# Weights' float64 words turned into float32 by a parametric ReLU on ScalarE, one shift and one OR

## The chip, the cores and the metric

The kernel runs on one core of a Trainium2 chip. The metric is the device time in microseconds of one launch. The time before is the median of three runs.

## The reference, cut to what matters

Sigmoid attention over 8 batches of 12 heads (448 positions, head width 64), then a two-layer perceptron over the 3584 tokens:

```
scores = matmul(q, k^T) / sqrt(64) - log(448)
x      = matmul(sigmoid(scores), v)          # 8 x 448 tokens, 768 wide
h      = x @ w_in                            # 768 -> 2048
g      = h where h >= 1; 0 where h <= -1; (h + 1)^2 / 4 between
out    = g @ w_out                           # 2048 -> 768
```

The two weight matrices reach the kernel as float64. The kernel computes in float32 and in pairs of float16 (a high and a low half), and so has to turn each float64 weight into a float32 first. A float64 is two 32-bit words. The high one holds the sign, 11 bits of exponent and 20 bits of mantissa; the low one's top three bits are the last that a float32 keeps.

## The kernel before, in words

**Stages.** The batches `b` follow each other. Each has six head pairs, and each pair four pieces (three blocks of 128 keys and a half block), so 24 pieces a batch. Per piece TensorE makes scores (lines 407, 411, 416 and 425), ScalarE makes the sigmoid (454 or 457) and TensorE multiplies by V (498). After a batch's pieces its x is copied out (504), its maximum is found (508, 517), spread over the partitions by a small matmul (165, 175, 176) and x is scaled and split into halves (521, 522). Then come the up products of the perceptron (`up`, line 722; from batch 2 on `up_blocks`, 688), the bend of `h` into `g` (735 to 739), and the down products (`down`, 758). While one batch goes through the perceptron, the next one's attention is worked in between. The first eight pairs are multiplied as float32 and need no split; they come from `first_qvk`.

**Weights.** Each matrix is 16 chunks of 128 rows by 768 float64, that is 768 KB each. `Weight.load` (line 202) starts a chunk's transfer: w_in's on the queue of SyncE, most of w_out's on ScalarE's. w_in's raw words lie in six spare places inside w_out's buffer, so the load of chunk f+6 waits until chunk f is converted, and what stands behind it on SyncE's queue waits too. `Weight.convert` (210) is called once per step and works on three chunks: it finishes chunk f-2, begins chunk f and does the middle of chunk f-1.

- Begin: ScalarE takes the absolute value of the high word, read as a float32 (line 224). For a *summed* chunk (the even ones of w_in) a clamp follows at once (226), on GpSimd for the first four and on VectorE for the other four.
- Middle, on VectorE: for a chunk that isn't summed, the clamp of line 236 also gives the maximum by an accumulator; then two shifts in one operation (241), the OR with the low word's top bits (244), and the OR with the sign and the top exponent bit out of the high word (247).
- Finish, for the summed chunks alone: ScalarE sums absolute values into an accumulator (218), which serves as a bound of the maximum.

There are 8 summed chunks and 24 others (8 of w_in, all 16 of w_out). `find_scale` is called twice for each matrix, after half its chunks and after all: it takes the maximum over chunks (259), makes a true float32 of it (262, 265), merges the sums (269), spreads the maximum over the partitions (165, 175, 176) and sets the scale (131 to 139). `split` then makes the float16 halves of each chunk (286 and 287, or 282 to 284 with GpSimd).

**Order.** Program order gives priorities, and a scheduler places each engine's instructions by them and by its own idea of when data is ready. What each engine runs in which order is therefore fixed when the kernel is built, for all engines at once, and a change of a few instructions can move others. Each engine works through its list in order: an instruction that waits holds up all behind it.

Of the kernel before, what the change touches and what calls it, by code (L numbers as in the profile page):

```python
# [14 lines left out]
F32 = mybir.dt.float32  # L15
F16 = mybir.dt.float16
BF16 = mybir.dt.bfloat16
I32 = mybir.dt.int32
AF = mybir.ActivationFunctionType
ALU = mybir.AluOpType  # L20
AX = mybir.AxisListType
PSUM = bass.MemoryType.PSUM

P = 128
# [4 lines left out]
ATT = 2.0**14  # L29
TINY = 2.0**-60  # L30

HIGH_MIN = 1.125 * 2.0**-15

NFULL = 8
NHALF = 6

# [17 lines left out]
LSTEP = 3  # L54

SB = 2
CLAMP = 7
QA = 17
QT = 3
WOP = 6  # L60
# [15 lines left out]
def sigmoid_attention_mlp(ctx: ExitStack, tc: tile.TileContext, first_qvk, qkv, w_in, w_out, out_t):  # L76
    nc = tc.nc
    NFULL, _, _, S = first_qvk.shape
    B = out_t.shape[1] // S
    NFC, _, DM = w_out.shape  # L80
# [44 lines left out]
    def scales(m, n, tag, pool=None, square=False, less=0):  # L125

        pool = pool or sml_p
        few = {"bufs": 1} if tag == "x" else {}
        mask, top = (EXP_MASK - EXP_ONE, TOP - 1) if square else (EXP_MASK, TOP - less)
        e = sml_p.tile([P, 3], F32, tag="e", name=tag + "_e")[:, :n]  # L130
        nc.vector.tensor_scalar(out=e, in0=m, scalar1=TINY, scalar2=None, op0=ALU.max)  # L131
        ei = e.bitcast(I32)
        nc.vector.tensor_scalar(out=ei, in0=ei, scalar1=mask, scalar2=None, op0=ALU.bitwise_and)
        s = pool.tile([P, n], F32, tag=tag + "_s", name=tag + "_s", **few)
        nc.vector.tensor_scalar(
            out=s.bitcast(I32), in0=ei, scalar1=-1.0, scalar2=float((2 * 127 + top) * EXP_ONE), op0=ALU.mult, op1=ALU.add
        )
        inv = pool.tile([P, n], F32, tag=tag + "_i", name=tag + "_i", **few)
        nc.vector.tensor_scalar(  # L139
            out=inv.bitcast(I32), in0=ei, scalar1=float(top * EXP_ONE), scalar2=None, op0=ALU.subtract  # L140
        )
        return s, inv
# [7 lines left out]
        out=ident, in_=ident, pattern=[[-1, P]], compare_op=ALU.is_equal, fill=0.0, base=0, channel_multiplier=1  # L150
# [17 lines left out]
    def all_max(m, diag=None):  # L168

        if diag is None:  # L170
            diag = on_diagonal(m)
            pm = ps_mo.tile([P, 512], F32, tag="mo", name="pm")
        else:
            pm = ps_sc.tile([P, 2, 512], F32, tag="psc", name="psc")[:, 0, :]
        nc.tensor.matmul(pm[:, :P], ones, diag, start=True, stop=True)
        nc.vector.tensor_reduce(out=m, in_=pm[:, :P], axis=AX.X, op=ALU.max)


    class Weight:
# [30 lines left out]
        def convert(self):  # L210

            f = self.at - 2
            if 0 <= f < NFC:
                w = self.words.pop(f)
                if f in self.summed:

                    dump = wo.f32(-1) if self is wi else w[:, :DM].bitcast(F32)
                    nc.scalar.activation(dump, self.f32(f), AF.Abs, accum_out=self.most[:, 1, f : f + 1])
                if self is wo:
                    self.load(3 if f == 3 else 1)  # L220
            f = self.at
            if f < NFC:
                a = self.f32(f)
                nc.scalar.activation(a, self.words_of(f)[1].bitcast(F32), AF.Abs)
                if f in self.summed:
                    (nc.vector if f >= CLAMP else nc.gpsimd).tensor_scalar(
                        out=a, in0=a, scalar1=HIGH_MIN, scalar2=None, op0=ALU.max
                    )
            f = self.at - 1
            if 0 <= f < NFC:  # L230

                low, high = self.words_of(f)
                a = self.f32(f)
                ai = a.bitcast(I32)
                if f not in self.summed:
                    nc.vector.tensor_scalar(
                        out=a, in0=a, scalar1=HIGH_MIN, scalar2=0.0, op0=ALU.max, op1=ALU.max,
                        accum_out=self.most[:, 0, f : f + 1],
                    )

                nc.vector.tensor_scalar(
                    out=ai, in0=ai, scalar1=5, scalar2=2, op0=ALU.logical_shift_left, op1=ALU.logical_shift_right
                )
                nc.vector.scalar_tensor_tensor(  # L244
                    out=ai, in0=low, scalar=29, in1=ai, op0=ALU.logical_shift_right, op1=ALU.bitwise_or
                )
                nc.vector.scalar_tensor_tensor(  # L247
                    out=ai, in0=high, scalar=-0x40000000, in1=ai, op0=ALU.bitwise_and, op1=ALU.bitwise_or
                )
                if self is wi:  # L250
                    self.load(1, nc.sync)
            self.at += 1

        def find_scale(self):

            k = len(self.scale)
            name = "%s%d" % (self.name, k)
            m = sml_p.tile([P, 2], F32, tag="wm", name=name + "_m", bufs=1)
            nc.vector.tensor_reduce(out=m, in_=self.most[:, :, GROUPS[k]], axis=AX.X, op=ALU.max)
            c, e = m[:, 0:1], sml_p.tile([P, 1], F32, tag="wx", name=name + "_x", bufs=1)  # L260
            ci, ei = c.bitcast(I32), e.bitcast(I32)
            nc.vector.tensor_scalar(
                out=ei, in0=ci, scalar1=5, scalar2=2, op0=ALU.logical_shift_left, op1=ALU.logical_shift_right
            )
            nc.vector.scalar_tensor_tensor(
                out=ei, in0=ci, scalar=0x40000000, in1=ei, op0=ALU.bitwise_and, op1=ALU.bitwise_or
            )

            nc.vector.tensor_scalar(
                out=e, in0=e, scalar1=float(DM // P), scalar2=m[:, 1:2], op0=ALU.mult, op1=ALU.max  # L270
            )
            all_max(e)
            s, inv = scales(e, 1, name, const, square=self is wo)
            self.scale.append(s)
            self.inv.append(inv)
# [552 lines left out]
    with tc.manual_schedule(engines={mybir.EngineType.SP}):  # L828
        load_pair(0)
        wi.load(1, nc.sync)  # L830
        load_pair(1)
        wi.load(2, nc.sync)
        load_pair(2)
        wi.load(3, nc.sync)
        for i in range(LAG):
            scores([i])
        state["scored"] = LAG
        while at < NPIECE:
            step(at)
            at += 1  # L840
            for what, when in ((load_pair, L0), (prep_a, A0), (prep_b, A0 + 1)):
                for k in range(2):
                    if at == when + LSTEP * k:
                        what(NFULL + k)
            convert(wi, min((NA + 1) * at // WI_A, NA + 1 + max(0, at - WI_A) * (NFC - NA) // (NPIECE - WI_A + WI_B)))
            if at == WI_A:
                with tc.high_priority(offset=WI_PRIO):
                    wi.find_scale()
                    wi.split(0)
                    wi.split(1)  # L850
# [7 lines left out]
    for u, unit in enumerate(units):  # L858
        while at < 2 * NPIECE and B0 + (at - NPIECE) * (B1 - B0) // NPIECE <= u:
            step(at)  # L860
            at += 1
        if wi.at < NFC + 1:
            n = NPIECE - WI_A
            convert(wi, NA + 1 + min(NFC - NA, (n + u + 1) * (NFC - NA) // (n + WI_B)))
            if wi.at == NFC + 1:
                wi.find_scale()
                group_scales(0, inv_x, 1)
        f, r = divmod(u, NCC // 2)

        assert all(at >= NPC * (p + 1) or (f + 1) * S * 4 <= slot_of(p) * 3 * S * 4 for p in range(NP, NFULL)), u  # L870
        if r == 0 and f < NFC:
            wi.split(f + AHEAD, f >= POOL_FROM)
        if wo.at < NA + 1:
            convert(wo, min(NA + 1, (u + 1) * (NA + 1) // WO_A))
            if wo.at == NA + 1:
                wo.find_scale()
                split_at = 0
        elif wo.at < NFC + 1:
            convert(wo, min(NFC + 1, NA + 1 + (u + 1 - WO_A) * (NFC - NA) // (WO_B - WO_A)))
            if wo.at == NFC + 1:  # L880
                wo.find_scale()
                roots()
        if len(wo.scale):
            while split_at < min(NA, 2 * (u + 1 - WO_A)):
                wo.split(split_at, split_at % WOP == 1)
                split_at += 1
        unit()
# [79 lines left out]
```

## Time and profile before

| | |
|---|---|
| time, three runs | 1190.55, 1190.84, 1192.1 us |
| median | 1190.84 us |
| span of the profiled execution | 1185.7 us |
| TensorE busy | 1144.9 us (97%) |
| VectorE, ScalarE, GpSimd busy | 854.9, 697.6, 332.8 us |
| mean granted TensorE clock | 0.991 |

The profile is of one execution more. Its span, from the first to the last instruction, is 1185.7 us; that execution's own device time isn't given beside it. The median stands 5.1 us above the span, which is what lies around the instructions. All sums are made against the span, and the 5.1 us are carried over as they are.

In the profile PE is TensorE (PEld its weight loads), DVE VectorE, ACT ScalarE, POOL GpSimd and SP SyncE; "L247" is line 247. A bracket at a row's end is the idle time of the engine before that row and what ended it. Operations in a row overlap a little at their ends, so that a 0.96 us operation holds the engine for some 0.87 us when the next follows directly.

### The profile page before, as it was taken

The page shows a single profiled execution, that of the slowest core. Times are in us where ns is not written, and L with a number is a line of the kernel's source. Part 1 is how long each engine was busy: PE and PEld are TensorE (multiplying, and loading weights), DVE is VectorE, ACT ScalarE, POOL GpSimd, SP SyncE. Part 2 cuts the span into 40 slices and gives each one's busy share as a digit, 9 for nine tenths or more (in the row PEclk, how much of TensorE's full clock was granted, in tenths as well). Part 3 has the DMA queues.
Part 4 walks back from the last instruction along what each step waited for, and adds up shares of the span by engine and source line. Part 5 has one row for each costly group of instructions (what it writes and reads, how often), then busy time and mean ns, then how long its engine had stood idle before and what let it go on. Part 6 is the DMA issues. An engine that isn't in the chain of part 4 may idle for free.

```text
span 1185.7 us, 20268 instructions
## 1 busy us (share of the span) xinstructions
PE 1144.9 (97%) x7662; PEld 669.3 (56%) x7662; DVE 854.9 (72%) x1828; ACT 697.6 (59%) x1158; POOL 332.8 (28%) x393
## 2 busy tenths in 40 slices
PE   5889899999999999999999999999999999999998
PEld 1224333444445776457754677557764577558954
DVE  6999999999956588457973689456884678736830
ACT  5886576665654577547864578455864476613510
POOL 3004410011323244234345235332532353310000
PEclk9899999999999999999999999999999999999999
DMA  9842354437542266224643065423552246302400
GB/s 367 322 153 76 118 161 152 134 119 257 182 148 72 95 217 210 76 72 142 238 163 102 30 236 208 135 64 128 204 211 64 65 147 220 126 24 87 163 16 32
DMA packets 58113, 170.01 MB, mean 143 GB/s; under 512 B 8608, under 2 KB 39840, under 8 KB 51872
## 3 DMA queue, kind: packets, MB, share of 16 engines
q1 hardware_dynamic: 56288, 159.29, 39.1%
q10 hardware_dynamic: 1728, 9.44, 2.2%
q8 instruction: 60, 0.98, 0.3%
q14 instruction: 37, 0.30, 0.1%
HBM read 126.94 MB, written 23.40 MB: 127 GB/s over the span
## 4 chain that ended last, share of the span: by engine, by line
PE 71%; DVE 17%; DMA 4%; ACT 3%; issue 2%; POOL 2%; SPq 0%; POOLq 0%; ACTq 0%; DVEq 0%
PE po L758 33%; PE ph L688 22%; PE pav L498 8%; PE psc L416 3%; PE psc L425 2%; PE ph L722 2%; DVE g L736 2%; PE psc L411 1%; DVE g L737 1%; DVE ghl L739 1%; DMA raw<-qkv 1%; DVE ahl L466 1%; DVE w_in_sb L244 1%; DVE mixa L632 1%; DVE w_out_sb L247 1%
## 5 line engine op out<-in xcount | busy, mean ns | idle before, releaser
L758 PE MATMUL po<-ghl,w_out_sb 128*128 128x448 f16 x2304 | 446.3, 353 | 1.5 <-DVE qkv_e L131 0.6
L758 PEld LDWEIGHTS <-w_out_sb 128*128 128x128 f16 x2304 | 221.7, 98 | 219.4 <-issue 15.9
L688 PE MATMUL ph<-w_in_sb 128*128 128x224 f16 x3024 | 307.7, 259 | 1.3 <-DVE g L737 0.9
L688 PEld LDWEIGHTS <-w_in_sb 128*128 128x128 f16 x3024 | 282.6, 98 | 30.1 <-issue 27.2
L466 DVE SCALAR_TENSOR_TENSOR ahl<-psc,ahl 128x896 f16<-128x896 f32 (+1 forms) x170 | 153.0, 900 | 105.7 <-ACT ahl L465 103.6
L378 POOL TENSOR_SCALAR raw<-raw,qkv_s 128x448 f32<-128x448 f32 (+1 forms) x93 | 71.0, 777 | 449.9 <-DVE qkv_i L139 346.3
L457 ACT ACTIVATE psc<-psc,nls,sqk 128x896 f32<-128x896 f32 (+1 forms) x136 | 129.5, 971 | 103.5 <-PE psc L425 86.6
L465 ACT ACTIVATE ahl<-psc 128x896 f16<-128x896 f32 (+1 forms) x170 | 126.9, 762 | 29.8 <-DVE ahl L466 28.6
L722 PE MATMUL ph<-xhl,w_in_sb 128*128 128x448 f16 x576 | 114.5, 356 | 4.7 <-DVE g L737 3.4
L344 ACT ACTIVATE dump<-raw 128x448 f16<-128x448 f32 (+1 forms) x105 | 61.9, 589 | 85.8 <-DMA raw<-qkv 84.5
L697 DVE TENSOR_TENSOR xhl<-ph,xhl 128x224 f32<-128x224 f32 x240 | 87.7, 383 | 25.3 <-PE ph L688 19.4
L738 ACT ACTIVATE ghl<-g 128x448 f16<-128x448 f32 x128 | 72.5, 573 | 44.2 <-DVE g L737 43.8
L498 PE MATMUL pav<-ahl,v 128*64 128x448 f16 x748 | 95.6, 360 | 0.0
L735 ACT ACTIVATE g<-xhl,hr,ihr 128x448 f32<-128x448 f32 x96 | 68.7, 752 | 41.9 <-DVE xhl L697 41.0
L722 PEld LDWEIGHTS <-w_in_sb 128*128 128x128 f16 x576 | 55.7, 99 | 63.6 <-issue 14.4
L736 DVE SCALAR_TENSOR_TENSOR g<-g,rk 128x448 f32<-128x448 f32 x112 | 81.4, 741 | 10.2 <-ACT g L735 10.0
L739 DVE TENSOR_TENSOR ghl<-g,ghl 128x448 f16<-128x448 f32 x128 | 85.0, 672 | 5.3 <-ACT ghl L738 4.8
L768 DVE TENSOR_SCALAR o<-po,od 128x448 f32<-128x448 f32 x48 | 32.5, 679 | 61.1 <-PE po L758 60.8
L380 POOL TENSOR_TENSOR hl<-raw,hl 128x448 f16<-128x448 f32 x62 | 71.1, 1167 | 0.0
L416 PE MATMUL psc<-qk 128*128 128x448 f16 x252 | 66.3, 354 | 2.0 <-ACT a L454 1.0
L737 DVE SCALAR_TENSOR_TENSOR g<-xhl,ihs,g 128x448 f32<-128x448 f32 x96 | 66.3, 708 | 0.3
L498 PEld LDWEIGHTS <-v 128*64 128x64 f16 x748 | 36.3, 109 | 37.9 <-issue 23.0
(167 smaller groups left out, 1198.5 us busy)
## 6 DMA issues: line engine op xcount, KB each, us to landing
w_in_sb<-blocks SPq DMA_DIRECT2D x48, 1344.0 KB, 6.1
raw<-qkv SPq DMA_DIRECT2D x34, 704.0 KB, 4.7
qk<-hl SPq DMA_DIRECT2D x320, 56.0 KB, 2.0
w_out_sb<-w_in SPq DMA_DIRECT2D x16, 768.0 KB, 8.5
out_t<-o SPq DMA_DIRECT2D x48, 224.0 KB, 1.9
blocks<-mixs SPq DMA_DIRECT2D x8, 768.0 KB, 3.5
w_out_sb<-w_out ACTq DMA_DIRECT2D x6, 768.0 KB, 4.1
raww<-w_out ACTq DMA_DIRECT2D x6, 768.0 KB, 5.7
```

Of the source, the lines that this page charges most:

```text
L416: nc.tensor.matmul(out, kq[:, j, 1, w], kq[:, j, 0, :], start=True, stop=False)
L457: nc.scalar.activation(a, a, AF.Sigmoid, bias=nls, scale=sqk)
L465: nc.scalar.activation(hi, x, AF.Copy, scale=ATT)
L466: nc.vector.scalar_tensor_tensor(out=lo, in0=x, scalar=ATT, in1=hi, op0=ALU.mult, op1=ALU.subtract)
L498: nc.tensor.matmul(pav[j * D : (j + 1) * D, :S], *terms[j][t], start=c == 0 and t == 0, stop=mid and t == len(terms[j]) - 1,)
L688: nc.tensor.matmul(out, w[:, wt, wh, c * P : (c + 1) * P], xc[:, xt, c, xh, :], start=j in (0, 2) and c + wh + xh == 0, stop=c == HC - 1 a ...
L697: add = lambda out, q, other: nc.vector.tensor_tensor(out=out, in0=quarter(q), in1=other, op=ALU.add)
L722: nc.tensor.matmul(ph[:, :S], w_in_sb[:, f, wh, c * P : (c + 1) * P], xhl[:, c, xh, :], start=c == 0 and wh + xh == 0, stop=c == NCC - 1 a ...
L736: nc.vector.scalar_tensor_tensor(out=g, in0=g, scalar=rt, in1=g, op0=ALU.min, op1=ALU.mult)
L737: nc.vector.scalar_tensor_tensor(out=g, in0=h, scalar=ihs, in1=g, op0=ALU.mult, op1=ALU.max)
L739: (nc.gpsimd if f % GPOOL else nc.vector).tensor_tensor(out=ghl[:, f, 1, :], in0=g, in1=hi, op=ALU.subtract)
L758: nc.tensor.matmul(po[:, :S], w_out_sb[:, f, wh, m * P : (m + 1) * P], ghl[:, f, gh, :], start=f == lo and wh + gh == 0, stop=f == hi - 1 ...
```

## The change

ScalarE's absolute value becomes a parametric ReLU with scale 2^-112 and, for negative values, the factor -2^32. For a positive weight the result's bits hold the wanted exponent and mantissa three places too low, with zeros above; for a negative one they hold a one besides, which a shift by three brings to the place of the sign. So one shift and one OR with the low word give the float32 with its sign. The clamps (lines 226 and 236) and the sign operation (247) are gone. The maximum of a chunk that isn't summed is now a reduction of its own, of absolute values, after the OR. `find_scale` finds true float32 maxima and drops two of its small operations. The sums of line 218 stay, and so do all loads and splits in program order; what the scheduler makes of it is shown in the prediction. Behind the changed part the line numbers of the changed kernel are 22 lower: line 407 of before is 385, 498 is 476, 722 is 700.

```diff
-HIGH_MIN = 1.125 * 2.0**-15
-CLAMP = 7
...
             if f < NFC:
-                a = self.f32(f)
-                nc.scalar.activation(a, self.words_of(f)[1].bitcast(F32), AF.Abs)
-                if f in self.summed:
-                    (nc.vector if f >= CLAMP else nc.gpsimd).tensor_scalar(
-                        out=a, in0=a, scalar1=HIGH_MIN, scalar2=None, op0=ALU.max
-                    )
+                high = self.words_of(f)[1].bitcast(F32)
+                nc.scalar.activation(self.f32(f), high, AF.Prelu, scale=2.0**-112, alpha=-(2.0**32))
             f = self.at - 1
             if 0 <= f < NFC:
-                low, high = self.words_of(f)
-                a = self.f32(f)
+                low, a = self.words_of(f)[0], self.f32(f)
                 ai = a.bitcast(I32)
-                if f not in self.summed:
-                    nc.vector.tensor_scalar(
-                        out=a, in0=a, scalar1=HIGH_MIN, scalar2=0.0, op0=ALU.max, op1=ALU.max,
-                        accum_out=self.most[:, 0, f : f + 1],
-                    )
-                nc.vector.tensor_scalar(
-                    out=ai, in0=ai, scalar1=5, scalar2=2, op0=ALU.logical_shift_left, op1=ALU.logical_shift_right
-                )
+                nc.vector.tensor_scalar(out=ai, in0=ai, scalar1=3, scalar2=None, op0=ALU.logical_shift_left)
                 nc.vector.scalar_tensor_tensor(
                     out=ai, in0=low, scalar=29, in1=ai, op0=ALU.logical_shift_right, op1=ALU.bitwise_or
                 )
-                nc.vector.scalar_tensor_tensor(
-                    out=ai, in0=high, scalar=-0x40000000, in1=ai, op0=ALU.bitwise_and, op1=ALU.bitwise_or
-                )
+                if f not in self.summed:
+                    nc.vector.tensor_reduce(
+                        out=self.most[:, 0, f : f + 1], in_=a, axis=AX.X, op=ALU.max, apply_absolute_value=True
+                    )
...
-            ci, ei = c.bitcast(I32), e.bitcast(I32)
             nc.vector.tensor_scalar(
-                out=ei, in0=ci, scalar1=5, scalar2=2, op0=ALU.logical_shift_left, op1=ALU.logical_shift_right
-            )
-            nc.vector.scalar_tensor_tensor(
-                out=ei, in0=ci, scalar=0x40000000, in1=ei, op0=ALU.bitwise_and, op1=ALU.bitwise_or
-            )
-            nc.vector.tensor_scalar(
-                out=e, in0=e, scalar1=float(DM // P), scalar2=m[:, 1:2], op0=ALU.mult, op1=ALU.max
+                out=e, in0=c, scalar1=float(DM // P), scalar2=m[:, 1:2], op0=ALU.mult, op1=ALU.max
             )
```

The change moves instructions on every engine, up to the middle of batch 1's perceptron; behind that TensorE's order is the same as before. Three places, where the order is read from the built programs and holds no times.

VectorE at the start, before: chunk 0 of w_in (summed, three rows), then chunk 1 (not summed, four rows; line 236 is the clamp with the maximum).

```order
L241 TENSOR_SCALAR w_in_sb<-w_in_sb 128x768
L244 SCALAR_TENSOR_TENSOR w_in_sb<-w_out_sb,w_in_sb 128x768
L247 SCALAR_TENSOR_TENSOR w_in_sb<-w_out_sb,w_in_sb 128x768
L236 TENSOR_SCALAR w_in_sb,wi_most<-w_in_sb 128x768
L241 TENSOR_SCALAR w_in_sb<-w_in_sb 128x768
L244 SCALAR_TENSOR_TENSOR w_in_sb<-w_out_sb,w_in_sb 128x768
L247 SCALAR_TENSOR_TENSOR w_in_sb<-w_out_sb,w_in_sb 128x768
```

The same place in the changed kernel (228 is the shift, 229 the OR, 233 the reduction):

```order
L228 TENSOR_SCALAR w_in_sb<-w_in_sb 128x768
L229 SCALAR_TENSOR_TENSOR w_in_sb<-w_out_sb,w_in_sb 128x768
L228 TENSOR_SCALAR w_in_sb<-w_in_sb 128x768
L229 SCALAR_TENSOR_TENSOR w_in_sb<-w_out_sb,w_in_sb 128x768
L233 TENSOR_REDUCE wi_most<-w_in_sb 128x1
```

Seven operations of two chunks became five, and the maximum moved from the front of its chunk to the back.

ScalarE behind its second table load, before: 454 is the sigmoid of a piece (`a` and a number), 224 the start of a chunk, 218 the sum of a summed chunk.

```order
L454 ACTIVATE a_123<-psc,nls 128x896
L454 ACTIVATE a_128<-psc,nls 128x896
L224 ACTIVATE w_in_sb<-w_out_sb 128x768
L218 ACTIVATE w_out_sb,wi_most<-w_in_sb 128x768
L224 ACTIVATE w_in_sb<-w_out_sb 128x768
L454 ACTIVATE a_133<-psc,nls 128x896
L454 ACTIVATE a_140<-psc,nls 128x448
L224 ACTIVATE w_in_sb<-w_out_sb 128x768 x2
L218 ACTIVATE w_out_sb,wi_most<-w_in_sb 128x768
```

In the changed kernel (432 is the sigmoid, 222 the parametric ReLU, 215 the sum):

```order
L432 ACTIVATE a_123<-psc,nls 128x896
L215 ACTIVATE w_out_sb,wi_most<-w_in_sb 128x768
L432 ACTIVATE a_128<-psc,nls 128x896
L222 ACTIVATE w_in_sb<-w_out_sb 128x768 x2
L432 ACTIVATE a_133<-psc,nls 128x896
L215 ACTIVATE w_out_sb,wi_most<-w_in_sb 128x768
L432 ACTIVATE a_140<-psc,nls 128x448
L222 ACTIVATE w_in_sb<-w_out_sb 128x768 x2
```

The sums of chunks 0 and 2 stand earlier among the sigmoids, the second of them before the half piece `a_140` and before the starts of chunks 3 and 4.

TensorE at the end of batch 0's attention, before: the row with `a_463` is the last product with V of batch 0; 407 are scores of batch 1's first two pairs, 175 spreads the maximum of x, 416 begins scores of the third pair.

```order
L498 MATMUL pav<-a_463,ghl 64x448 x2
L407 MATMUL psc<-ghl 128x448 x2
L498 MATMUL pav<-a_496,ghl 64x448 x2
L407 MATMUL psc<-ghl 128x448 x2
L498 MATMUL pav<-a_688,ghl 64x448 x2
L407 MATMUL psc<-ghl 128x448 x2
L175 LDWEIGHTS one
L175 MATMUL pm<-diag,one 128x128
L407 MATMUL psc<-ghl 64x448 x2
L416 LDWEIGHTS qk
L416 MATMUL psc<-qk 128x448
```

Two pieces of lines 416 and 425 in all follow there, and then the first up product, line 722. In the changed kernel (`a_442` is the last of batch 0; 172 spreads the maximum, 385 are scores, 476 products with V, 700 is the first up product):

```order
L476 MATMUL pav<-a_442,ghl 64x448 x2
L172 LDWEIGHTS one
L172 MATMUL pm<-diag,one 128x128
L385 MATMUL psc<-ghl 128x448 x2
L476 MATMUL pav<-a_475,ghl 64x448 x2
L385 MATMUL psc<-ghl 128x448 x2
L476 MATMUL pav<-a_660,ghl 64x448 x2
L700 LDWEIGHTS w_in_sb
L700 MATMUL ph<-xhl,w_in_sb 128x448
```

The small matmul of the maximum now stands directly behind batch 0's last product with V, and the up products (36 in a row) begin ahead of four score pieces that stood before them: a full and a half one of line 407, and two of lines 416 and 425. A second small matmul of the same line, for w_in's second scale, stands behind those 36.

## The prediction

> **What bounds the kernel now.** I read the page's totals first, then the busy time by stage. In the rows of the stages stand the stretch in us and its length, then busy time and instructions of PE, PEld, DVE, ACT and POOL, then the granted clock, the DMA share and GB/s.
>
> ```profile
> PE 1144.9 (97%) x7662; PEld 669.3 (56%) x7662; DVE 854.9 (72%) x1828; ACT 697.6 (59%) x1158; POOL 332.8 (28%) x393
> ```
>
> ```profile
> 0.00:15.00 15.00, 7.02 (x18) 2.16 (x20) 3.88 (x10) 7.36 (x9) 2.83 (x7) 1.00 0.88 326
> 15.00:45.00 30.00, 20.34 (x70) 5.18 (x70) 29.16 (x47) 20.79 (x33) 6.83 (x3) 0.80 1.03 406
> 45.00:75.00 30.00, 26.13 (x113) 7.03 (x111) 29.57 (x61) 29.12 (x45) 0.00 (x0) 0.97 0.69 232
> 75.00:91.70 16.70, 14.10 (x57) 3.57 (x55) 15.72 (x34) 11.32 (x15) 0.00 (x0) 0.90 0.26 95
> 91.70:330.00 238.30, 227.55 (x1182) 102.25 (x1181) 225.79 (x454) 157.04 (x248) 49.72 (x41) 0.99 0.44 147
> 330.00:1185.70 855.70, 849.75 (x6232) 549.12 (x6229) 550.80 (x1227) 471.93 (x813) 273.43 (x342) 1.00 0.37 128
> ```
>
> TensorE bounds the whole: it idles 1185.7 - 1144.9 = 40.8 us. Of these 24.1 lie before 91.7 (67.6 busy in the four rows), where the up products begin, 10.8 between 91.7 and 330, and 6.0 behind. The weights are converted in the first two of these stretches, so this change can win at most some 35 us of idle time, and what the lower clock costs: 20.34 busy at 0.80, 26.13 at 0.97 and 14.10 at 0.90 are 4.1 + 0.8 + 1.4 = 6.3 us of full-speed work lost.
>
> In the first stage three things are full by turns: from 15 to 45 the DMA (share 1.03) and VectorE (29.16 of 30), from 45 to 75 VectorE (29.57) and ScalarE (29.12). Who waits for whom says which ends last. First TensorE, then ScalarE, both over the first stage (total, times, longest):
>
> ```profile
> PE psc L407 <- ACT a L454: 14.4, 7, 3.5
> PE psc L407 <- DMA ghl<-first_qvk: 4.5, 1, 4.5
> PE pm L175 <- DVE diag L165: 2.6, 1, 2.6
> PE pav L498 <- ACT x L504: 2.5, 2, 2.3
> ```
>
> ```profile
> ACT w_out_sb L218 <- DVE w_in_sb L247: 8.6, 5, 2.7
> ACT w_in_sb L224 <- DMA w_out_sb<-w_in: 7.4, 4, 6.0
> ACT a L454 <- PE psc L407: 4.1, 3, 2.6
> ACT w_in_sb L286 <- DVE w_in_sb L287: 1.8, 1, 1.8
> ```
>
> TensorE waits for sigmoids (14.4) and for x's copy (2.5), both ScalarE's. ScalarE in turn stands 8.6 us in its sums of line 218, waiting for line 247, the very operation that goes; the sigmoids queued behind them come late. Of the stage between, TensorE's two largest waits:
>
> ```profile
> PE ph L722 <- DVE g L737: 3.4, 3, 1.8
> PE pm L159 <- DVE g L737: 3.2, 2, 2.6
> ```
>
> Both name VectorE, which is busy 225.79 of 238.30 us there.
>
> **The change part by part.** *VectorE's work.* What goes, and the two reductions from which the new one's price comes (minimum, median, maximum in ns):
>
> ```profile
> L247 DVE SCALAR_TENSOR_TENSOR w_in_sb<-w_out_sb,w_in_sb x16: 937/957/1460, 12.8 to 73.0; 128x768 int32<-128x768 int32 x16
> L247 DVE SCALAR_TENSOR_TENSOR w_out_sb<-w_out_sb x10: 945/960/2397, 78.0 to 162.4; 128x768 int32<-128x768 int32 x10
> L247 DVE SCALAR_TENSOR_TENSOR w_out_sb<-raww,w_out_sb x6: 944/954/959, 144.6 to 194.6; 128x768 int32<-128x768 int32 x6
> ```
>
> ```profile
> L236 DVE TENSOR_SCALAR_CACHE_REDUCE w_out_sb<-w_out_sb x16: 936/949/959, 67.6 to 187.1; 128x768 f32<-128x768 f32 x16
> L236 DVE DVE_READ_ACCUMULATOR w_out_sb<-w_out_sb x16: 76/86/97, 68.5 to 188.0; 128x1 f32 x16
> ```
>
> ```profile
> L226 POOL TENSOR_SCALAR w_in_sb<-w_in_sb x4: 2124/2126/2579, 9.0 to 25.7; 128x768 f32<-128x768 f32 x4
> L226 DVE TENSOR_SCALAR w_in_sb<-w_in_sb x4: 553/560/562, 35.1 to 60.3; 128x768 f32<-128x768 f32 x4
> ```
>
> ```profile
> L508 DVE TENSOR_REDUCE xm<-x x48: 600/609/625, 30.9 to 1055.9; 128x1 f32<-128x448 f32 x48
> ```
>
> ```profile
> L346 DVE TENSOR_REDUCE m<-raw x2: 676/881/1086, 985.5 to 986.5; 128x2 f32<-128x896 f32 x1, 128x1 f32<-128x512 f32 x1
> ```
>
> Line 247: 32 x 0.957 = 30.6 us. The clamp on VectorE: 4 x 0.56 = 2.2. The maximum: 609 ns for 448 elements and 1086 for 896 make 1.065 ns an element, so 768 cost 609 + 320 x 1.065 = 950 ns, against 949 and a read of 86 that mostly overlaps; I take 0.05 us won in each of 24, 1.2 in all, with 0.09 and nothing as ends. Of the three small operations of each `find_scale` two go, well under 0.2 us each: 1.2 for the four. In all 35 us of the 304 that VectorE is busy in the first 330, 22.5 of them before 91.7 (20 chunks of 32, all the clamps). The shift stays at the price of the double shift: the one-operation clamp in line 226's row is as fast as any.
>
> A rule speaks against the swap of the maximum: the Trainium skill, "VectorE: DVE Perf Modes", "Rules for kernel authors", expects only the plain rate of a `tensor_reduce` and advises to restructure. Were the old operation in the fast rate of line 226, the swap would cost 24 x 0.39 = 9.4 us and leave 24 of the 35 won; line 236's row, at 949 ns, has the plain rate already, so the trace does not bear that out.
>
> Another bears on line 247: the Trainium skill, "SBUF — State Buffer", "Who interferes with whom", has a VectorE instruction with two inputs in SBUF contend with GpSimd's reads, and a `tensor_reduce` never. The rows agree: line 247 reaches 2397 ns at a median of 960, line 236 never over 959. By it the 30.6 is the low end.
>
> *ScalarE.* The parametric ReLU isn't in the trace.
>
> ```profile
> L224 ACT ACTIVATE w_in_sb<-w_out_sb x16: 889/908/938, 8.1 to 61.2; 128x768 f32<-128x768 f32 x16
> ```
>
> I keep 0.91 us, the same operands and size. Both programs have two table loads, so no further one is needed. The nearest bounds are 0.89 to 0.94 in this row; a rival below takes double.
>
> *Who gains from it before 91.7.* A summed and an unsummed chunk together hold VectorE for 0.56 + 0.96 + 0.56 + 0.96 + 0.95 = 4.0 us (shift, OR, shift, OR, maximum) where it was 6.0 (two operations of 0.96 more and the read), and GpSimd's 2.13 in front is gone. Four terms of TensorE's idle time:
>
> (a) Sigmoids and x: 14.4 + 2.5 = 16.9. The longest wait, 3.5 at the start, stands behind a table load and the first chunk and stays. Of the 13.4 left, ScalarE's waits for VectorE (8.6 + 1.8 = 10.4) are the reachable part. They don't all go: the sums now stand earlier on ScalarE (the order rows) and so ask VectorE earlier, and the DMA holds the start of chunks:
>
> ```profile
> 24.76 0.90 ACT L224 ACTIVATE w_in_sb<-w_out_sb 128x768 f32<-128x768 f32 x1 [0.25 <-DMA w_out_sb<-w_in]
> 25.57 0.99 ACT L454 ACTIVATE a<-psc,nls 128x896 f32<-128x896 f32 x1
> 29.24 0.84 ACT L218 ACTIVATE w_out_sb<-w_in_sb 128x768 f32<-128x768 f32 x1 [2.68 <-DVE w_in_sb L247]
> ```
>
> At 24.76 a chunk begins as its transfer lands: nothing before it can be earlier than the DMA. The 2.68 behind it are VectorE's and go. From 45 on ScalarE has no idle time to win (29.12 of 30). I take 6 us; ends 2 (only VectorE's late part) and 10.
>
> (b) The small matmuls: 2.6 goes, since two of the chain's small steps are gone and VectorE's list has one conversion step between them where it had six. The one for x now stands directly behind the last product with V and waits for the copy, the reduction of 0.61 and three short steps. I take 1.8, so 0.8 won; ends -3 and 2.6.
>
> (c) The clock: 6.3 us are lost to it, in the stretches with gaps. With a third of the gaps gone I take 1.5; ends 0 and 4.
>
> (d) The tail. Today x's last reduction begins at 82.21, and the up products at 91.74:
>
> ```profile
> 82.21 0.62 DVE L508 TENSOR_REDUCE xm<-x 128x1 f32<-128x448 f32 x1
> ...
> 86.80 0.26 DVE L165 TENSOR_SCALAR diag<-ident,xm 128x128 bf16<-128x128 bf16 x1
> ```
>
> ```profile
> 91.74 0.55 PE L722 MATMUL ph<-xhl,w_in_sb 128*128 128x448 f16 x2
> ```
>
> Much of these 9.5 us, and most of the 4.8 to line 165's end, are conversions ahead of x's small steps on VectorE. But TensorE fills them with pieces, four of which come behind the first up products now. So the up products may start 11 or 12 us sooner, and some 3.4 us of that is only moved: it is no term of its own.
>
> *Between 91.7 and 330* VectorE has 12.7 us less to do. One wait shows the mechanism:
>
> ```profile
> 137.86 2.40 DVE L247 SCALAR_TENSOR_TENSOR w_out_sb<-w_out_sb 128x768 int32<-128x768 int32 x1
> ```
>
> ```profile
> 143.50 0.16 PE L159 MATMUL pm<-mb,one 128*128 128x2 bf16 x1 [2.58 <-DVE g L737]
> ```
>
> A bend's step (737) stood behind a stretched line 247, and TensorE waited 2.58. This goes. I take (e) 2.5 us; the ends are 6 (most of the two rows' 6.6) and -3, since the order here is new on all engines and w_out's loads, some on ScalarE's queue, move with it. On SyncE's queue loads of raw pairs and w_out change places with the small qk copies; nobody on TensorE waits for these by the rows above. Behind 330 the order is the same: 0.
>
> Sum: 6 + 0.8 + 1.5 + 2.5 = 10.8, so 11. Span 1185.7 - 11 = 1174.7; with the 5.1 us that lie between span and median, **1180**. All upper ends make 22.6 (1168), all lower ones -4 (1195).
>
> **The rivals.** *Held elsewhere.* The DMA to 45 us and ScalarE from 45 to 75 set the pace, and VectorE's 22.5 us become idle time. Then (a) is 2 and the rest nothing: 1189. For it: 1.03 and 29.12. Against: ScalarE idles 9.2 of the 30 us to 45, and 8.6 of its waits name line 247.
>
> *Slower, by the new order on TensorE.* The small matmul for x stands with nothing between it and the last V product, and 36 up products stand before pieces that once filled the wait. If VectorE is as far behind as today, the 4.8 us from 82.21 to that matmul's input all show, once more 2.6 at the second such matmul, and (e) ends at its -3: 10.4 lost. The 2.6 that goes and (a) at 2 are 4.6 won: 5.8 longer, 1197. It decides from the point where new waits exceed the 10 that (a), (c) and (e) bring. Against: VectorE has 22.5 us less by then.
>
> *The ReLU takes double.* 20 of 32 fall in the first stage: 18 us on the engine that is full there, 1198; it decides from 0.55 us more each. Nothing in the trace speaks for it.
>
> The Trainium skill, "ScalarE: Activation LUTs", "Step-by-step: what each stage is for", has one element a cycle whatever the function; no run here shows it for this one yet.
>
> *It does not save what it says:* a single integer shift at the plain rate, 0.95 and not 0.56, gives back 32 x 0.39 = 12.5 of the 35; the gain shrinks by the same third, to 7: 1184.
>
> *More than thought:* (a), (c) and (e) near their upper ends, about 20: 1171.
>
> **How the numbers follow.** Forecast 0.67; held elsewhere 0.11; new order 0.08; double ReLU 0.03; slow shift 0.04; more 0.07. The range 1172 to 1190 leaves out the two slower ones and the largest gain, 0.18. About 0.2% (2.4 us) is what a measurement can tell. Faster: 0.67 + 0.04 + 0.07 = 0.78. The same: 0.10 of held elsewhere's 0.11. Slower: 0.08 + 0.03 and the 0.01 left of it, 0.12.
>
> **What would show it.** Right: ScalarE's wait in the sums from 8.6 to under 4; TensorE's idle before the up products from 24.1 to about 16; the first up product near 80; the new reductions at 0.95 and the ReLU at 0.91; no 2.6 us wait near 140. Wrong: waits for the DMA on ScalarE growing by what those for VectorE lose (held elsewhere); a wait over 4 us at the small matmul of x (new order); ScalarE's ReLU over 1.4 us; shifts at 0.95; or new waits of TensorE between 91.7 and 330.

## The result, and the profile after

The changed kernel takes 1183.27 us (median of 4 runs, 1182.14 to 1185.21) against 1191.42 of the kernel before (4 runs); the ratio is 0.9936 with a 95% interval of 0.9922 to 0.995. It is faster: 8.2 us by the medians, where 11 were forecast (1180, range 1172 to 1190). Most of the reasons, though, did not hold.

The page's totals of the changed kernel (line 407 of before is 385 here, 498 is 476, 722 is 700):

```profile
PE 1146.3 (97%) x7662; PEld 669.0 (57%) x7662; DVE 824.9 (70%) x1760; ACT 697.1 (59%) x1158; POOL 321.6 (27%) x389
```

The same stages as in the prediction (busy PE, PEld, DVE, ACT, POOL; granted clock, DMA share, GB/s):

```profile
0.00:15.00 15.00, 6.28 (x16) 1.98 (x16) 2.15 (x7) 7.44 (x9) 0.70 (x6) 0.89 0.86 316
15.00:45.00 30.00, 24.03 (x90) 6.10 (x90) 24.46 (x45) 23.95 (x40) 0.00 (x0) 0.83 1.03 406
45.00:75.00 30.00, 22.28 (x83) 5.89 (x81) 26.12 (x43) 26.98 (x40) 0.00 (x0) 0.85 0.76 264
75.00:91.70 16.70, 16.70 (x76) 5.31 (x73) 10.46 (x28) 11.50 (x17) 0.00 (x0) 0.95 0.16 48
91.70:330.00 238.30, 231.76 (x1196) 102.60 (x1195) 217.43 (x429) 158.20 (x250) 47.11 (x42) 0.99 0.48 159
330.00:1181.30 851.30, 845.29 (x6210) 547.09 (x6208) 544.26 (x1212) 469.07 (x807) 273.80 (x342) 1.00 0.37 125
```

TensorE's idle time went from 40.8 to 35.0 us: before 91.7 only from 24.1 to 22.4 (69.3 busy now), between 91.7 and 330 from 10.8 to 6.5, behind it 6.0 as before. TensorE's busy time grew by 1.4. That is the 4.4 us between the two spans, 1185.7 and 1181.3.

TensorE's waits up to 91.7, then from 91.7 to 330 (total, times, longest):

```profile
PE psc L385 <- ACT a L432: 17.1, 8, 4.2
PE psc L385 <- DMA ghl<-first_qvk: 4.5, 1, 4.5
PE pav L476 <- ACT x L482: 0.5, 2, 0.3
```

```profile
PE ph L700 <- DVE xhl L500: 2.9, 1, 2.9
PE ph L700 <- DVE g L715: 1.9, 1, 1.9
PE po L736 <- DVE g L715: 0.9, 1, 0.9
PE psc L389 <- DVE ahl L444: 0.4, 1, 0.4
```

The 2.6 us at the small product of w_in's first scale (at 42.38 us in the kernel before) and the 2.6 near 140 are gone. The wait for sigmoids has grown from 14.4 to 17.1, and a new one of 2.9 stands at x's second split. ScalarE's and VectorE's waits of the first stage:

```profile
ACT w_in_sb L222 <- DMA w_out_sb<-w_in: 6.7, 1, 6.7
ACT w_out_sb L215 <- DVE w_in_sb L229: 5.7, 4, 2.4
ACT w_out_sb L222 <- DMA w_out_sb<-w_out: 3.6, 3, 2.7
```

```profile
DVE w_in_sb L228 <- ACT w_in_sb L222: 16.3, 5, 8.7
```

VectorE now waits for ScalarE, 16.3 us, of which 8.7 are the start, where VectorE of before waited 10.1 for GpSimd's first clamp; ScalarE waits for w_out's transfers, 3.6. The prices (minimum, median, maximum in ns):

```profile
L222 ACT ACTIVATE w_in_sb<-w_out_sb x16: 876/910/941, 8.8 to 58.3; 128x768 f32<-128x768 f32 x16
L228 DVE TENSOR_SCALAR w_out_sb<-w_out_sb x16: 546/560/1305, 63.3 to 180.1; 128x768 int32<-128x768 int32 x16
L229 DVE SCALAR_TENSOR_TENSOR w_out_sb<-w_out_sb x10: 948/956/1571, 63.9 to 152.6; 128x768 int32<-128x768 int32 x10
L233 DVE TENSOR_REDUCE wo_most<-w_out_sb x16: 940/946/953, 64.9 to 184.3; 128x1 f32<-128x768 f32 x16
```

The ReLU costs what the absolute value did, the shift 560 ns, the reduction 946.

### The profile page after: what moved, and what is told of

Same layout as the page of the kernel before. It is cut to its first block, busy times and chain, and to the rows that moved or that the text cites. A ratio compares the mean times of both kernels' runs of the same rounds, so it can differ in the third digit from the quotient of the medians.

```text
span 1181.3 us, 20203 instructions
## 1 busy us (share of the span) xinstructions
PE 1146.3 (97%) x7662; PEld 669.0 (57%) x7662; DVE 824.9 (70%) x1760; ACT 697.1 (59%) x1158; POOL 321.6 (27%) x389
## 4 chain that ended last, share of the span: by engine, by line
PE 76%; DVE 9%; DMA 8%; ACT 4%; issue 1%; POOL 1%; SPq 0%; ACTq 0%; DVEq 0%
PE po L736 35%; PE ph L666 23%; PE pav L476 8%; PE psc L394 3%; PE psc L403 3%; DMA blocks<-mixs 2%; PE ph L700 2%; DMA w_out_sb<-w_in 2%; PE psc L389 1%; DMA raw<-qkv 1%; ACT a L432 1%; DVE g L714 1%; DMA w_out_sb<-w_out 1%; DMA w_in_sb<-blocks 1%; DVE mixs L624 1%
## 5 line engine op out<-in xcount | busy, mean ns | idle before, releaser
L700 PEld LDWEIGHTS <-w_in_sb 128*128 128x128 f16 x576 | 55.9, 99 | 64.0 <-issue 16.4
L714 DVE SCALAR_TENSOR_TENSOR g<-g,rk 128x448 f32<-128x448 f32 x112 | 81.1, 739 | 10.7 <-ACT g L713 10.5
L385 PE MATMUL psc<-ghl 64*128 64x448 f32 (+1 forms) x128 | 37.4, 672 | 21.9 <-ACT a L432 17.1
```

What stands on the lines that cost most here:

```text
L700: nc.tensor.matmul(ph[:, :S], w_in_sb[:, f, wh, c * P : (c + 1) * P], xhl[:, c, xh, :], start=c == 0 and wh + xh == 0, stop=c == NCC - 1 a ...
L714: nc.vector.scalar_tensor_tensor(out=g, in0=g, scalar=rt, in1=g, op0=ALU.min, op1=ALU.mult)
```

## The experiments

Theory at first: the gain is VectorE's freed time. Rivals: something else holds the first stage, and, later, that the gain belongs to the order of the instructions, which the scheduler makes anew for each kernel. Ratios are to the kernel before, measured beside it on the same chip.

**The kernel before again**, unchanged.

> The kernel before once more, as a zero and for a second profile. Its own profile had a span 5.1 us under the median of its runs, while the changed kernel's runs all stand 1.7 us above their spans. If the 1.7 holds for every kernel, the first profile was of an execution some 3.4 us shorter than the median, and this one's span should lie near 1189. If the 5.1 belongs to this kernel, the span is 1186 again. Ratio 1.000 within 0.002.

Measured: 1192.74 us, 12 runs from 1188.11 to 1196.07, ratio 1.0012 [0.9998, 1.0027]. The profiled execution has a span of 1192.3 us and took 1193.99, 1.7 us more. So the instructions' surroundings cost 1.7 us, not 5.1, and the first profile of before (span 1185.7) shows an execution some 3.4 us shorter than the median.

**One more VectorE operation on all 32 chunks**, **on w_out's 16 alone**, **on w_in's 16 alone**: an AND with zero, ORed in.

```diff
+                nc.vector.scalar_tensor_tensor(
+                    out=ai, in0=self.words_of(f)[1], scalar=0, in1=ai, op0=ALU.bitwise_and, op1=ALU.bitwise_or
+                )
                 if f not in self.summed:
```

> The changed kernel with one operation more per chunk on VectorE, an OR with the high word masked to zero: the same form and size as the removed sign operation, without effect on the values. If the gain is VectorE's time (theory), 32 x 0.957 = 30.6 us of it are back and the time is 1188 to 1192. If it comes from the shorter way at the start (no GpSimd clamp, no clamps at all) and the order that follows from it (rival), the extra operation costs little: 1183 to 1186.

> The same extra operation for w_out's 16 chunks alone. By the profile after, the idle time of TensorE before the up products fell by about 2 us only and that between 91.7 and 330 us by 4, so if the gain is won while w_out is converted (theory) most of it is lost here: 1187 to 1190. If it is won while w_in is converted (the prediction's own view, two thirds before the up products), 1183 to 1186.

> The changed kernel with one more VectorE operation of some 0.95 us, which alters nothing, on each of the 16 chunks of w_in alone (w_out's stay as changed). Theory: while w_in is converted TensorE waits for ScalarE, not for VectorE, so VectorE's time is cheap there: the first up product moves back from 87.5 to 88-91 us and the time stays at 1183-1187 us, ratio to before 0.993-0.997, against the 10.7 us that the same operation costs on w_out's chunks. Rival: VectorE's time is worth as much on w_in as on w_out, so that half of the 11 us that all 32 operations cost comes back here: 1188-1190 us, ratio 0.997-1.000.

Measured: all, 1194.25 us, ratio 1.0028 [1.0015, 1.0041]; w_out, 1193.95, 1.0023 [1.0006, 1.004]; w_in, 1188.97, 0.999 [0.9979, 1.0002]. The first looked like a yes to the theory, though it and the second lie above the times that the theory gave (1188 to 1192 and 1187 to 1190), and the third lies in its rival's. Taken together the three are none: 28.0, 13.3 and 10.1 us more of VectorE's busy time cost 11.0, 10.7 and 5.7 us, so the parts do not add up, and w_in's chunks are not cheap as expected. Besides, each of the three has an order of its own: by the traces, a product of another kind than in the changed kernel stands at 285 to 346 of the 7662 places in TensorE's list of products.

**w_out's loads earlier**, to end ScalarE's 3.6 us wait for them: two chunks go to other free places, and the first loads are issued two conversions sooner. TensorE's order stays as it is.

```diff
-    wo = Weight(w_out, w_out_sb, "wo", [13, 15, 9, 11, 13, 15, 9, 11, 0, 0, 13, 15, 0, 0, 0, 0])
+    wo = Weight(w_out, w_out_sb, "wo", [13, 15, 5, 7, 13, 15, 9, 11, 0, 0, 13, 15, 0, 0, 0, 0])
...
-            if w is wi and w.at in (NFC - 3, NFC + 1):
+            if w is wi and w.at in (NFC - 3, NFC - 1):
```

> The changed kernel with w_out's chunks 2 and 3 loaded two chunks sooner, into places that come free sooner. In the profile after, ScalarE stood 2.67 us for chunk 2's transfer with a sigmoid behind it, TensorE waited 3.59 for that sigmoid and then ran eight products in 3.25 us that take 1.72 at full clock. If this new wait ate the first stage's gain (theory), 1178 to 1181. If what is won there is lost again at the next wait for VectorE or in moved pieces (rival), 1182 to 1184.

Measured: 1183.04 us, ratio 0.9933 [0.9916, 0.995]: nothing gained over the changed kernel, as the rival had it. ScalarE's wait for w_out's loads shrank from 3.6 to 1.4 us, and TensorE's wait for sigmoids is no shorter for it:

```profile
PE psc L385 <- ACT a L432: 19.6, 12, 4.8
```

It is 17.1 in the changed kernel's profile, but 18.9 to 21.7 in four further profiles that have the same lists of instructions up to there (MIX0 12 and the three reordered kernels below), so 19.6 is no growth either.

**No sums on ScalarE for w_in**, alone and with w_out's loads earlier. VectorE takes the maxima instead.

```diff
-WI_SUM = 2
+WI_SUM = 0
```

> The changed kernel with the absolute sums of w_in's 7 or 8 summed chunks taken off ScalarE (0.93 us each) and made reductions on VectorE (0.95 us each). Theory: ScalarE sets the first stage since the change (VectorE waits 16.3 us for the ReLUs there), so TensorE's waits for ScalarE's a fall from 17.1 us to 8-13 and the first up product comes at 83-86 us in place of 87.5; the time is 1177-1182 us, ratio 0.989-0.993. Rival 1: VectorE is still the bound: first up product at 89-91, time 1185-1189. Rival 2: the first stage gains, but the wait for x's split near 218 us takes it back: 1182-1185.

> The same without sums on w_in, and w_out's first four chunks loaded ahead of w_in's end into free places, as in the run before that did this alone. Theory: both of ScalarE's waits and its work fall, first up product at 81-85 us, time 1175-1180 us, ratio 0.987-0.991, below the kernel without sums by 1-3 us. Rival: the load is hidden anyway: the same time as without sums, within 1 us.

Measured: 1190.86 us, ratio 1.0005 [0.9995, 1.0015], and 1190.54, 1.0004 [0.9992, 1.0016]. The first up product comes at 85.9 and 85.0 us, earlier than the changed kernel's 87.5, as the theory of a first stage held by ScalarE had it. Yet the end is 7 us later: the block products that begin batch 2 start at 398.8 and 399.0 in place of 390.4. What the first stage gains is lost behind it; the second rival's direction, but far beyond its 1182 to 1185. With w_out's loads earlier besides, the time is the same within 1 us, as that run's rival had it. TensorE's two longest gaps behind 91.7 in the first of the two:

```profile
222.99 9.81 PE L700 MATMUL ph<-xhl,w_in_sb 128*128 128x448 f16 x51 [2.99 <-DVE xhl L500]
240.50 0.16 PE L156 MATMUL pm<-mb,one 128*128 128x3 bf16 x1 [4.39 <-DVE g L715]
```

The wait for x's split is there as in the changed kernel, and 4.39 us at a pair's small product are new.

**Mixing begun later.** Mixing is the work on VectorE and ScalarE that makes the blocks of weights for `up_blocks` out of w_in's chunks; MIX0 is the unit of work at which it begins. TensorE's 2.9 us wait at 218 us stands behind VectorE's wait for a buffer of the mixing.

```diff
-MIX0 = 8
+MIX0 = 12
```

> The changed kernel with the mixing of w_in's chunks begun at unit 12 in place of 8 (the six steps lie closer). Theory: the 2.93 us wait of TensorE for x's split at 218 us is made by mix's buffer, which waits 1.72 us for the store of mixs with the split queued behind it on VectorE; with the mixing later the wait in the trace is below 1 us, the slow products behind it are gone, and the time falls by 2-5 us to 1178-1181, ratio 0.989-0.992. Rival: VectorE's queue is as full, another operation of it is late near 218, or the later mixing delays the block products at 390 us: 1182-1187.

Measured: 1182.8 us, ratio 0.9945 [0.9925, 0.9965]. The number moved nothing: every engine's order is as in the changed kernel. So the run tells nothing of the mixing; it is the changed kernel once more, and repeats its time.

By now the picture was suspicious: the three kernels with TensorE's order of the changed kernel stood at 1182.8 to 1183.3, and every other at some 1189 or more, however much VectorE did. The next runs change only the order. No instruction is added or removed: WO_A is the unit by which w_out's first conversions are due, B1 the one by which the heads' steps in the first batch's products end.

**The changed kernel in another order**, **the kernel before with the same number**, and **the changed kernel in a third order**.

```diff
-WO_A = 42
+WO_A = 41
```

```diff
-B1 = 66
+B1 = 67
```

> The changed kernel with the same instructions on every engine, in another order: w_out's first conversions are due one unit earlier (WO_A 41 in place of 42), which moves some 650 of TensorE's 14,798 rows and some 410 of VectorE's, none of TensorE's ahead of row 523. Theory A (the gain is VectorE's freed time, whatever the order): 1181-1186 us, ratio 0.992-0.996. Theory B (the order that the cheaper conversion led to holds the gain; any order near it gives it up again, as the four kernels with more VectorE work and an order of their own did at 1189-1194): 1188-1195 us, ratio 0.998-1.004, with waits of TensorE for g, x's split or v between 120 and 400 us that the changed kernel doesn't have.

> The kernel before with the same instructions in another order, by the same number (WO_A 41): some 670 rows of TensorE and 160 of VectorE move. Theory A: 1189-1193 us, ratio 0.998-1.002, as VectorE's work is the same. Theory B: the order alone moves the time by several us either way, 1183-1199.

> The changed kernel with the same instructions in a third order (the heads' steps in the first batch's products end one unit later, B1 67 in place of 66; some 450 rows of TensorE and 370 of VectorE move). Theory A: 1181-1186 us, ratio 0.992-0.996. Theory B: 1188-1195 us, ratio 0.998-1.004.

Measured: the changed kernel with WO_A 41, 1191.87 us, ratio 1.0009 [0.9994, 1.0024]; before with WO_A 41, 1191.94, 1.0032 [1.0016, 1.0048]; the changed kernel with B1 67, 1189.02, 0.9991 [0.9975, 1.0006]. Theory A, VectorE's freed time whatever the order, falls: with all of that time still saved, the gain is gone. At WO_A 41 the medians of the changed kernel and of the one before are 0.07 us apart; by the ratios the changed one is 0.2% the shorter, with intervals that overlap. The kernel before loses some 0.3% by this order. The first of them, TensorE's waits from 91.7 to 330 and that stage:

```profile
PE ph L700 <- DVE xhl L500: 3.0, 1, 3.0
PE pm L156 <- DVE mb L153: 2.6, 1, 2.6
PE ph L700 <- DVE g L715: 2.6, 3, 1.4
PE pm L156 <- DVE g L715: 2.2, 1, 2.2
PE psc L389 <- POOL v L358: 1.2, 1, 1.2
```

```profile
91.70:330.00 238.30, 226.61 (x1154) 99.27 (x1152) 210.53 (x413) 152.96 (x239) 46.37 (x41) 0.98 0.45 149
```

TensorE idles 11.7 us there, where it was 6.5. And VectorE idles 238.3 - 210.5 = 27.8, where it was 12.5 in the kernel before (16.2 in its second profile) and 20.9 in the changed one. The freed time became VectorE's idle time, and the waits for VectorE stayed.

**x's second split first.** The same instructions in a fourth order, meant to take away the one wait over 2 us that the changed kernel has behind 91.7.

```diff
-    inv_x = finish_x(1)
-    common_scales(1, inv_x)
+    with tc.high_priority(offset=50):
+        inv_x = finish_x(1)
+        common_scales(1, inv_x)
```

> The changed kernel with x's scale and split of the second batch given precedence, so that on VectorE they stand ahead of the mixing that waits for its buffer, and the maximum's small product stands 18 rows earlier on TensorE; nothing ahead of that place moves, 126 rows of TensorE do behind it. Theory (x's split queued behind the mixing on VectorE is what TensorE waits for near 218 us): the wait of 2.93 us falls below 1 us, the slow products behind it go, 1178-1181 us, ratio 0.989-0.992. Rival (any other order gives the gain up, whatever wait it is made for): another wait of 2 us or more appears between 205 and 400 us and the time is 1184-1192, ratio 0.994-1.001.

Measured: 1190.0 us, ratio 0.9999 [0.998, 1.0018]. The wait is gone; of the following five the ones of lines 700 and 389 have grown from 1.9 and 0.4, and the other three are new:

```profile
PE ph L700 <- DVE g L715: 3.3, 3, 2.2
PE psc L394 <- DVE qkv_e L128: 2.3, 1, 2.3
PE psc L389 <- DVE ahl L444: 1.7, 1, 1.7
PE pm L156 <- DVE g L715: 1.7, 1, 1.7
PE pav L476 <- ACT a L432: 1.6, 1, 1.6
```

The rival was right. No version beat the changed kernel clear of noise: the two with its order on TensorE have medians 0.2 and 0.5 us lower.

**Where the orders part.** Two marks from each timeline, the start of the first up product and of batch 2's first block product (behind it all need 790.6 to 793.2 us more):

| kernel | time, us | first up | block | between |
|---|---|---|---|---|
| before, two profiles | 1189.6 to 1192.7 (medians) | 91.7, 91.0 | 394.5, 400.6 | 302.8, 309.6 |
| before, WO_A 41 | 1191.9 | 92.8 | 396.9 | 304.1 |
| changed | 1183.3 | 87.5 | 390.4 | 302.9 |
| w_out earlier (same order on TensorE) | 1183.0 | 87.0 | 390.5 | 303.5 |
| MIX0 12 (same order) | 1182.8 | 89.9 | 392.3 | 302.3 |
| changed, WO_A 41 | 1191.9 | 88.4 | 399.4 | 311.0 |
| changed, B1 67 | 1189.0 | 87.1 | 396.0 | 308.9 |
| changed, x first | 1190.0 | 86.8 | 396.4 | 309.6 |
| no sums; and w_out earlier | 1190.9; 1190.5 | 85.9; 85.0 | 398.8; 399.0 | 312.9; 314.0 |
| extra on all; w_out; w_in | 1194.3; 1194.0; 1189.0 | 90.5; 87.9; 87.5 | 403.0; 398.8; 397.2 | 312.5; 310.9; 309.7 |

The earlier first up product is real and holds in every order of the changed kernel: 86.8 to 89.9 where before has 91.0 to 92.8. What lies between the marks takes 302 to 304 us in the changed kernel's own order and 309 to 314 in the eight others with the new conversion. The kernel before shows 302.8 and 309.6 with one and the same order, so the mark of one profile can be off by as much.

One place tells the three good kernels from all the others. Near 280 us the sums of a freshly loaded pair of heads (line 322) and the split of the pair before it (351) follow on ScalarE. In the changed kernel the split stands first; ScalarE's rows, and the load's issue on SyncE's queue:

```profile
274.55 1.23 ACT L351 ACTIVATE hl<-raw,qkv_s 128x448 f16<-128x448 f32 x2 [1.47 <-DVE qkv_i L136]
275.69 0.70 ACT L351 ACTIVATE v<-raw,qkv_s 128x512 f16<-128x512 f32 x1
276.30 0.56 ACT L322 ACTIVATE dump<-raw 128x448 f16<-128x448 f32 x1
```

```profile
271.00 0.39 SPq L306 DMA_DIRECT2D raw<-qkv  x1
```

In the order with WO_A 41 the sum stands first and waits for its load; the split, and VectorE behind it, wait with it:

```profile
283.75 0.58 ACT L322 ACTIVATE dump<-raw 128x448 f16<-128x448 f32 x1 [3.36 <-DMA raw<-qkv]
...
285.03 1.21 ACT L351 ACTIVATE hl<-raw,qkv_s 128x448 f16<-128x448 f32 x2
```

```profile
278.50 0.39 SPq L306 DMA_DIRECT2D raw<-qkv  x1
```

```profile
285.71 0.69 DVE L352 SCALAR_TENSOR_TENSOR hl<-raw,qkv_s,hl 128x448 f16<-128x448 f32 x1 [3.11 <-ACT hl L351]
```

ScalarE has this wait for the load, 1.6 to 5.1 us, in all eleven profiles of other orders, those of before among them (2.6, 2.2 and, at WO_A 41, 2.6), and in none of the three good ones. (Later waits for such loads, near 343 and 363 us, the good ones have too.) In six kernels (w_in's extra, both without sums, the three reordered) VectorE then loses 3.1 to 4.8 us to the split. So it marks the kernels. But it does not carry the loss in general: before has the wait too, with stretches of 302.8 and 304.1 in two of its three profiles. And TensorE is late ahead of this place already. It has the same 1126 products ahead of the following row in the changed kernel, at WO_A 41, at B1 67 and with x first, in this order:

```profile
269.40 9.25 PE L736 MATMUL po<-ghl,w_out_sb 128*128 128x448 f16 x48
278.46 9.25 PE L736 MATMUL po<-ghl,w_out_sb 128*128 128x448 f16 x48
274.30 9.25 PE L736 MATMUL po<-ghl,w_out_sb 128*128 128x448 f16 x48
270.50 9.25 PE L736 MATMUL po<-ghl,w_out_sb 128*128 128x448 f16 x48
```

At WO_A 41 it is 9.1 us late there, which is all of the 9.0 at batch 2's first block product; at B1 67 4.9 of 5.6; only with x first do most of the 6.0 (all but 1.1) come behind this row. Ahead of it the kernel with WO_A 41 waits for VectorE 2.65 us at 140.93, 2.18 at 241.70 and 1.36 at 243.22, none of which the changed kernel has. Why VectorE is late at these places, though it has time to spare, is open. Shown is that the order alone moves this kernel by 6 to 9 us.

## Why the prediction was right, and where it failed

*The prices* held: 0.91 for the ReLU, 0.56 for the shift, 0.95 for the reduction. VectorE's busy time fell by 854.9 - 824.9 = 30.0 us of the 35 forecast, with none of it lost to the swap of the maximum. Part of the missing 5 may be the overlap of operations in a row, since the 35 counted each at its full length (32 of line 247 at some 0.09 us less would be 2.9); no run shows it by itself. By the Trainium skill, "ScalarE: Activation LUTs", "Step-by-step: what each stage is for", the function doesn't matter to the rate of an element; the trace now agrees, 910 ns against 908.

*(a) sigmoids and x, 6 us:* failed. The two waits were 16.9 and are 17.6. Further profiles agree: 16.4 and 17.5 for before, 19.4 to 22.2 for the first stage of the changed kernel. The first up product comes 4.2 us earlier, not 11 or 12, and with 2.5 us less work of TensorE done ahead of it (67.6 us busy up to 91.7, 65.1 up to 87.5). The step behind it was that ScalarE's waits for VectorE "are the reachable part": of 8.6 only 2.9 went, 3.6 came for transfers, and VectorE stands idle for 16.3 in front of the ReLUs, 7.6 of them behind the start. In this stage the rival "held elsewhere" fits best: VectorE's time became idle time, while TensorE goes on waiting for ScalarE. Taking ScalarE's wait for the transfers away, or its sums, gained nothing at the end.

*(b) the small products, 0.8:* 2.6, its upper end: the wait at w_in's first scale is gone, and x's product, though it stands directly behind the last product with V, waits for nothing. The rival "new order on TensorE" put the slow case here, and it did not come.

*(c) the clock, 1.5:* not seen. By the four rows 0.7 + 4.1 + 3.3 + 0.8 = 9.0 us are lost now where it was 6.3. But worked out in the same way, four more profiles with the same lists up to there (MIX0 12, WO_A 41, B1 67, x first) give 7.5, 6.7, 3.8 and 6.1, and the second one of before 6.0: neither a gain nor a loss is clear of this spread.

*(d) the tail:* no term, rightly, but the mark near 80 failed. x's last reduction begins at 80.81 and waited 2.56 for ScalarE's copy:

```profile
80.81 0.62 DVE L486 TENSOR_REDUCE xm<-x 128x1 f32<-128x448 f32 x1 [2.56 <-ACT x L482]
81.47 0.16 DVE L495 TENSOR_REDUCE xm<-xm 128x1 f32<-128x6 f32 x1
81.66 0.26 DVE L162 TENSOR_SCALAR diag<-ident,xm 128x128 bf16<-128x128 bf16 x1
```

Behind it all is as short as thought; ahead of it ScalarE is as late as before.

*(e) from 91.7 to 330, 2.5:* 4.2 here, inside its ends of -3 and 6, and the wait at 140 went. But the 10.8 us that it is counted from are no fixed mark. The second profile of before, the same lists of instructions in an execution 6.6 us longer, has 238.3 - 221.4 = 16.9 in this stage:

```profile
91.70:330.00 238.30, 221.36 (x1145) 99.15 (x1145) 222.11 (x447) 152.86 (x241) 50.51 (x41) 0.99 0.44 147
```

And the runs show that this is no worth of the 12.7 us that VectorE is spared: in three other orders with the same instructions TensorE's idle time there is 11.7, 8.7 and 10.8 in place of 6.5. "The order here is new on all engines" stood in the prediction as a reason for a lower end, not as the cause that decides.

*The 5.1 us around the span* were 1.7, and 3.4 of an execution that happened to be short. Of the 11 us forecast, 4.4 came by the spans; the medians differ by 8.2 because the first profile flattered the kernel before. The forecast landed 3.3 us off with two errors of opposite sign in it: the span was put 6.6 us too low, and what lies around it 3.4 too high.

By the prediction's own signs the account leans the same way. Of those for "right" the prices and the wait near 140 came; ScalarE's wait in the sums (5.7 for under 4), TensorE's idle time before the up products (22.4 for 16) and the first up product (87.5 for 80) did not. Of those for "wrong" two came: ScalarE's waits for the DMA grew by 2.9 us (7.4 to 6.7 + 3.6), as much as those in the sums lost, and TensorE has the new wait of 2.9 at 218.

So the step that failed is the one from VectorE's time to TensorE's: 30 us less of VectorE's work was taken to shorten TensorE's waits, and in three orders out of four it did not. That the time fell into the range is luck twice over: by the errors that cancel, and by the order that came out, the best of the four that were tried on the changed kernel. For the conversion as such the forecast should have been "about the same", with several us either way for the order.

## What to carry to other kernels

Where a scheduler makes the order, an edit brings a new order with it, and that may be worth more than the edit: before a gain or a loss is put down to freed work, move one due time by one, with the work left alone, and see how far the time moves. Adding work back is no clean test there, since it draws another order; here it seemed to confirm a theory that three runs with the work unchanged overturned. And take what lies around the span from one execution's own time and span, not from another's median.

## What the runs showed of the hardware

After some gaps of 3 us TensorE's next products are slow. In the changed kernel eight products of one form take 1.72 us, and 3.25 soon after a wait of 3.59:

```profile
61.42 1.72 PE L476 MATMUL pav<-a,ghl 128*64 128x448 f32 x8 [0.29 <-ACT x L482]
...
72.27 0.98 PE L385 MATMUL psc<-ghl 64*64 64x448 f32 x4 [3.59 <-ACT a L432]
73.18 3.25 PE L476 MATMUL pav<-a,ghl 128*64 128x448 f32 x8
```

So are the up products after the 2.93 us at 218: 18 of them in 6.11 us, 0.34 each, and later 33 in 6.42, 0.19 each.

```profile
218.10 6.11 PE L700 MATMUL ph<-xhl,w_in_sb 128*128 128x448 f16 x18 [2.93 <-DVE xhl L500]
...
224.81 6.42 PE L700 MATMUL ph<-xhl,w_in_sb 128*128 128x448 f16 x33
```

These two gaps cost more than their length: 18 products at 0.19 would have taken 3.5 us, 2.6 less, so the 2.93 cost 5.5; the 3.59 cost 5.1. It isn't so behind every gap. After 1.88 us in the same profile 36 products run at full pace, 0.19 each:

```profile
318.85 6.97 PE L700 MATMUL ph<-xhl,w_in_sb 128*128 128x448 f16 x36 [1.88 <-DVE g L715]
```

From which length on a gap is followed by slow products these runs don't show.

One kernel's executions also lie further apart than the differences asked about: before ran from 1186.4 to 1195.95 us in 29 executions, the changed kernel with MIX0 12 from 1178.63 to 1186.34 in 6, and the profiled one of a kernel can be any of these. One profile of each is therefore not enough for differences of 2 us.
